# Shared PSUM banks, an earlier third pair of loads, and one more seven-part product in a fused retention and feed-forward kernel

**Chip, cores, metric.** One core of one Trainium2 chip. The time is the device time of a launch in microseconds (us); the kernel before takes 290.7 us.

## The reference

Retention (attention with a decay in place of the softmax) over 8 batches, 8 heads, 576 positions of 64 channels; its 4608 rows of 512 go through a feed-forward layer 512 -> 2048 -> 512 with a squared ReLU.

```python
scores = scale * np.matmul(q, k.transpose(0, 1, 3, 2))
Dmat = np.where(rel >= 0, gamma[:, None, None] ** rel[None, :, :], 0.0)
attn_out = np.matmul(scores * Dmat[None], v)
x = attn_out.transpose(0, 2, 1, 3).reshape(B * S, H * D)
h = x @ w_in
r = np.maximum(h, 0.0)
out = (r * r) @ w_out
```

## The kernel before

The rows are cut into 36 units of 128, two to a group: 18 groups. For each group TensorE computes the retention (scores `psc`, sums of the recurrent state `psS`, outputs `psO`: many small products with 64 rows), then the first feed-forward product (`ph`, 128x256 products) and the second (`po`). VectorE masks the scores, scales the outputs to `xT` and adds; ScalarE does ReLU and square; GpSimd casts the loaded q and v. The first eight units are loaded as four pairs (k0 to v6), between the eight weight blocks of 1 MB (w0 to w3 of `w_in`, w4 to w7 of `w_out`).

The order on every engine is fixed when the kernel is built. A small scheduler inside it walks through tasks with assumed durations, a key (smaller goes first), dependencies, and counts of buffers that a task must acquire:

```python
sched = Schedule(dict(ff=4, prS=1, prO=1, g=3, ld=5, wst=4, ...))
FIRST = ["k0","q0","v0","k2","q2","v2","w0","w1","w2","w3","w4","w5","w6","w7","k4","q4","v4","k6","q6","v6"]
```

The eight PSUM banks are four single ones for the feed-forward layer and two fixed pairs, one for scores and sums, one for outputs and sums:

```python
ps_ff  = ctx.enter_context(tc.tile_pool(name="ps_ff",  bufs=4, space=bass.MemoryType.PSUM))
ps_ret = ctx.enter_context(tc.tile_pool(name="ps_ret", bufs=1, space=bass.MemoryType.PSUM))
...
def emit_scores(g):
    tile_of["psc", g] = ps_ret.tile([P, 2, 512], FP32, name="psc", tag="prS")
    ...
def after_scores(g, t, key):                  # mask on VectorE, one unit of the group at a time
    for s, u in enumerate(units_of(g)):
        ...
        m = add("DVE", key + s, 0.7, fm, deps=[t] + ..., acq=("rT",))
    sched.free("prS", [m])
...
t = add("PE", base + 3, ..., fa, deps=scores_deps(g) + sums_deps(g), acq=("prS", "prO") if nf else ("prS",))
after_scores(g, t, base + 5)                  # a group whose scores are not joined to another's outputs
```

The loads wait for one another by a helper (`behind`), so that they share the transfers in a chosen order:

```python
if (name, u) == ("k", 4):
    behind(t, tile_of["w", 5])               # third pair's k is issued when w5 has landed
...
if i == 0:
    behind(tile_of["w", i], tile_of["load", "v", 0])
```

The second product has two forms. Up to group `STRASSEN` it is 16 products of 128x512 for each unit. From there on it is Strassen's seven half-size products instead of eight: seven parts of eight 128x256 products, for which VectorE forms sums `gS` of the activations and, once, differences `wT` of the weights. Each part adds into a bank a, b or c:

```python
if STRASSEN <= g:                             # STRASSEN = 2: groups 0 and 1 take the plain form
    add_strassen(g, us, base2, sq)
    return
...
def product(k, key, bank, left, right, deps, start, stop, reads):
    for q in range(4):
        def f(q=q):
            if start and q == 0:
                tile_of["pb", g, bank] = ps_ff.tile([P, HM], FP32, name="po", tag="ff")
            for i in (2 * q, 2 * q + 1):
                nc.tensor.matmul(tile_of["pb", g, bank], lhsT=left(i), rhs=right[:, i, :], ...)
        last[:] = [add("PE", base + key + q, 0.2184, f, deps=..., acq=("ff",) if start and q == 0 else ())]
```

## Time and profile before

| | before |
|---|---|
| time, median | 290.71 us (290.68 to 290.76) |
| span of the profiled run | 289.1 us |
| TensorE busy | 282.1 us, 98% |
| first feed-forward product starts | 17.74 us |
| last run of small products starts | 254.02 us |
| last run of products starts | 283.78 us |

TensorE is the bound; the lines are in the prediction below. "Busy" hides small gaps, since pipelined products overlap. So the accounts here use the timeline of TensorE: the start of one run of products minus the start of the next is what the first run cost, with all that it waited. Between fixed points of the same content (the start of the first feed-forward product at 17.74 us, and the end of the last run of small products at 254.95; some expectations below call this stretch "from 17.3") the kernel before takes 237.21 us: 209.65 are large products at 0.109 us for 256 columns and 0.216 for 512, with 32 transposes; 23.95 lie in 34 runs of small products; 3.74 are 34 times 0.11, the prediction's figure for what the return to large products costs, taken over and not measured one by one; nothing but rounding (-0.13) is left. A run of small products with the return to large ones is called an excursion.

### The profile page before, as it was taken

How to read it: one execution, taken by the hardware profiler on the slowest of the kernel's cores; microseconds unless marked ns; L12 is line 12 of the kernel's file. 1: busy time of each engine (PE TensorE's matmuls, PEld its weight loads, DVE VectorE, ACT ScalarE, POOL GpSimd, SP SyncE). 2: the span in 40 equal slices, each digit the busy share in tenths (PEclk: the TensorE clock that was granted, in tenths of full speed). 3: DMA queues.
4: the chain of work that ended last, by engine and by line, in shares of the span. 5: the costliest groups of instructions: out<-in, count | busy, mean ns of one | idle time of the engine just before them, and what ended most of it. 6: DMA issues, size and time to landing. Idle time of an engine off the chain costs nothing.

```text
span 289.1 us, 9988 instructions
## 1 busy us (share of the span) xinstructions
PE 282.1 (98%) x4322; PEld 234.3 (81%) x4322; DVE 182.4 (63%) x381; ACT 188.2 (65%) x361; POOL 84.1 (29%) x121
## 2 busy tenths in 40 slices
PE   8999999999999999999999999999999999999994
PEld 3568755788888888888888888888888888888883
DVE  3772368769585657736686857575777775455622
ACT  5459964685757676767756767676767676747830
POOL 5660035443333243342506061505250500000000
PEclk9999999999999999999999999999999999999999
DMA  7999999999999689999788799899995920201004
GB/s 202 274 208 206 249 291 267 219 203 202 221 188 198 153 201 199 217 219 219 154 199 168 172 194 205 163 196 206 225 182 151 181 76 2 75 2 73 2 8 139
DMA packets 139436, 49.94 MB, mean 173 GB/s; under 512 B 118144, under 2 KB 135040, under 8 KB 139392
## 3 DMA queue, kind: packets, MB, share of 16 engines
q1 hardware_dynamic: 134848, 44.84, 75.3%
q0 software_dynamic: 4224, 4.19, 8.8%
q8 instruction: 34, 0.56, 0.8%
q10 hardware_dynamic: 320, 0.26, 0.4%
q14 instruction: 10, 0.08, 0.1%
HBM read 36.70 MB, written 9.44 MB: 160 GB/s over the span
## 4 chain that ended last, share of the span: by engine, by line
PE 91%; DMA 3%; issue 2%; POOL 2%; DVE 0%; POOLq 0%; DVEq 0%
PE ph L859 44%; PE po L951 34%; PE po L899 5%; PE psO L345 4%; DMA w_in<-in_moe_w_in_dram 3%; PE psc L345 2%; PE psS L345 2%; PE psT L423 1%; POOL mask L215 0%; POOL vx L404 0%; POOL w_in L319 0%; DVE o L974 0%; POOL mask L207 0%; DVE p L1003 0%; POOL mask L211 0%
## 5 line engine op out<-in xcount | busy, mean ns | idle before, releaser
L859 PE MATMUL ph<-xT,w_in 128*128 128x256 f16 x1152 | 139.9, 273 | 0.1
L859 PEld LDWEIGHTS <-w_in 128*128 128x128 f16 x1152 | 110.9, 98 | 14.8 <-DMA w_in<-in_moe_w_in_dram 0.3
L867 ACT ACTIVATE rl<-ph 128x512 f16<-128x512 f32 x144 | 84.5, 588 | 52.5 <-PE ph L859 50.9
L877 ACT ACTIVATE gT<-rl 128x512 f16<-128x512 f16 x118 | 74.4, 631 | 3.4
L951 PEld LDWEIGHTS <-gS 128*128 128x128 f16 x512 | 49.8, 98 | 5.9
L951 PE MATMUL po<-wT,gS 128*128 128x256 f16 x384 | 52.1, 273 | 0.0
L928 DVE TENSOR_TENSOR gS<-gT,gS 128x512 f16<-128x512 f16 x64 | 32.8, 517 | 14.2 <-ACT gT L877 13.5
L951 PEld LDWEIGHTS <-gT 128*128 128x128 f16 x384 | 37.1, 98 | 4.5
L928 DVE TENSOR_TENSOR gS<-gT 128x512 f16<-128x512 f16 x64 | 30.9, 485 | 12.6 <-ACT gT L877 12.5
L359 POOL CAST kq<-k 128x512 f16<-128x512 f32 x28 | 18.6, 663 | 61.4 <-DMA k<-in_k_dram 60.2
L951 PE MATMUL po<-w_out,gT 128*128 128x256 f16 x256 | 34.7, 273 | 0.0
L371 POOL TENSOR_TENSOR v<-v,vdec_full 128x512 f16<-128x512 f32 x24 | 25.4, 1057 | 21.9 <-DMA v<-in_v_dram 20.9
L359 POOL CAST kq<-q 128x512 f16<-128x512 f32 x28 | 18.5, 660 | 30.8 <-DMA q<-in_q_dram 30.6
L964 ACT COPY u<-po 128x256 f32<-128x256 f32 x32 | 11.8, 369 | 19.1 <-PE po L951 18.9
L974 DVE TENSOR_TENSOR o<-po,u 128x256 f32<-128x256 f32 x31 | 13.0, 420 | 16.3 <-PE po L951 10.0
L736 DVE TENSOR_TENSOR xT<-psO,gam_full 128x512 f16<-128x512 f32 x28 | 18.1, 684 | 6.3 <-PE psO L345 6.2
L682 DVE TENSOR_TENSOR rT<-psc,mask 128x512 f16<-128x512 f32 x28 | 18.3, 683 | 4.6 <-PE psc L345 4.5
L879 DVE TENSOR_TENSOR gT<-rl 128x512 f16<-128x512 f16 x26 | 12.8, 492 | 12.6 <-ACT rl L867 11.9
L974 DVE TENSOR_TENSOR o<-po,p 128x256 f32<-128x256 f32 x17 | 7.2, 423 | 17.8 <-ACT u L964 8.8
L951 PE MATMUL po<-wT,gT 128*128 128x256 f16 x128 | 16.8, 273 | 0.0
L951 PE MATMUL po<-w_out,gS 128*128 128x256 f16 x128 | 16.8, 273 | 0.0
L899 PE MATMUL po<-w_out,gT 128*128 128x512 f16 x64 | 15.7, 380 | 0.0
(78 smaller groups left out, 224.0 us busy)
## 6 DMA issues: line engine op xcount, KB each, us to landing
out_dram<-o SPq DMA_DIRECT2D x32, 256.0 KB, 3.7
k<-in_k_dram SPq DMA_DIRECT2D x24, 256.0 KB, 4.8
q<-in_q_dram SPq DMA_DIRECT2D x24, 256.0 KB, 5.1
v<-in_v_dram SPq DMA_DIRECT2D x24, 256.0 KB, 4.9
pair<-in_k_dram SPq DMA_DIRECT2D x4, 512.0 KB, 7.0
pair<-in_q_dram SPq DMA_DIRECT2D x4, 512.0 KB, 7.2
pair<-in_v_dram SPq DMA_DIRECT2D x4, 512.0 KB, 7.0
w_in<-in_moe_w_in_dram POOLq DMA_DIRECT2D x4, 512.0 KB, 8.9
```

Source lines behind the costliest of these rows:

```text
L345: t = nc.tensor.matmul(out_, lhsT=lhsT, rhs=rhs, start=start, stop=True, skip_group_check=True, tile_position=(64 * row, 64 * col))
L359: op(out=out_.rearrange("p (n b a d) -> p n b a d", n=2, b=2, a=2), in_=in_.rearrange("p (n a b) d -> p n b a d", n=2, a=2))
L371: nc.gpsimd.tensor_tensor(out=t, in0=tile_of["v32", u], in1=vdec[kind].rearrange("p (h o) -> p h o", o=1).to_broadcast([P, H, D]), op=ALU. ...
L682: tile_of["masking", g] = nc.vector.tensor_tensor(out=r, in0=tile_of["psc", g][:, :, cols(s)].rearrange("p a (n i) -> p a n i", i=64), in1 ...
L736: nc.vector.tensor_tensor(out=tile_of["x", g][:, :, s * P:(s + 1) * P].rearrange("p n (c i) -> p c n i", c=2), in0=tile_of["psO", g][:, :, ...
L859: nc.tensor.matmul(tile_of["ph", g, fb][:, j, :], lhsT=w_in16[:, m, fi * P:(fi + 1) * P], rhs=tile_of["x", g][:, m, :], start=(m == 0), st ...
L867: nc.scalar.activation(out=t, in_=tile_of["ph", g, fb], func=ACTF.Relu)
L877: nc.scalar.activation(out=t, in_=rl, func=ACTF.Square)
L899: nc.tensor.matmul(tile_of["po", u], lhsT=tile_of["g", g][:, fi, s * P:(s + 1) * P], rhs=w_out16[:, fi, :], start=(fi == 0), stop=(fi == N ...
L928: nc.vector.tensor_tensor(out=Sx(k, h), in0=in0(h), in1=in1(h), op=op)
L951: nc.tensor.matmul(tile_of["pb", g, bank], lhsT=left(i), rhs=right[:, i, :], start=(start and i == 0), stop=(i == HF - 1), skip_group_chec ...
L974: nc.vector.tensor_tensor(out=o_tile(u)[:, half * HM:(half + 1) * HM], in0=bank(x), in1=tile_of[name, g], op=ALU.add)
```

## The change

The intent: one more group gets the cheaper second product; for that all eight weight blocks and their differences must be there while other work still fills TensorE, so the third pair's loads move ahead of w3; and any free PSUM bank may serve any purpose.

```diff
-    STRASSEN = 2
+    STRASSEN = 1
-    ps_ff  = ...tile_pool(name="ps_ff", bufs=4, space=PSUM)
-    ps_ret = ...tile_pool(name="ps_ret", bufs=1, space=PSUM)
+    ps_ff  = ...tile_pool(name="ps_ff", bufs=8, space=PSUM)
-    FIRST = [... "w0","w1","w2","w3","w4","w5","w6","w7","k4","q4","v4","k6","q6","v6"]
+    FIRST = [... "w0","w1","w2","k4","q4","v4","w3","w4","w5","w6","w7","k6","q6","v6"]
+    AFTER = {0: ("v", 0), 3: ("k", 4), ("k", 4): 0, ("k", 6): 5}   # who is issued behind whose landing
-    sched = Schedule(dict(ff=4, ..., rT=4, ...))
+    sched = Schedule(dict(ff=8, ..., rT=2, ...))
+    def banks(name):
+        return [ps_ff.tile([P, 512], FP32, name=name, tag="ff") for i in range(2)]
-            if (name, u) == ("k", 4):
-                behind(t, tile_of["w", 5])
+            if (name, u) in AFTER:
+                behind(t, tile_of["w", AFTER[name, u]])
-            if i == 0:
-                behind(tile_of["w", i], tile_of["load", "v", 0])
+            if i in AFTER:
+                behind(tile_of["w", i], tile_of[("load",) + AFTER[i]])
-        tile_of["psc", g] = ps_ret.tile([P, 2, 512], FP32, name="psc", tag="prS")
+        tile_of["psc", g] = banks("psc")
# after_scores: one mask per bank (both units), each frees its bank
-        for s, u in enumerate(units_of(g)):
+        for a in range(2):
+            m = add("DVE", key + a, 0.7, fm, deps=..., acq=() if a else ("rT",))
+            sched.free("ff", [m])
# (sums, outputs and their scaling likewise; acq lists gain "ff","ff" per pair of banks) ...
```

More of the change, by code (lines that the diff above doesn't have):

```diff
@@ L152 @@
     r_pool = ctx.enter_context(tc.tile_pool(name="r", bufs=3))
-    ps_ff = ctx.enter_context(tc.tile_pool(name="ps_ff", bufs=4, space=bass.MemoryType.PSUM))
-    ps_ret = ctx.enter_context(tc.tile_pool(name="ps_ret", bufs=1, space=bass.MemoryType.PSUM))
+    ps_ff = ctx.enter_context(tc.tile_pool(name="ps_ff", bufs=8, space=bass.MemoryType.PSUM))
     ctx.enter_context(tc.manual_schedule())
@@ L234 @@
     PAIRED = 8
-    SHARED = ()
-    FIRST = ["k0", "q0", "v0", "k2", "q2", "v2", "w0", "w1", "w2", "w3", "w4", "w5", "w6", "w7", "k4", "q4", "v4", "k6", "q6", "v6"]
-    sched = Schedule(dict(ff=4, prS=1, prO=1, g=3, ld=5, wst=4, kq=7, v16=7, rT=4, x=3, rl=3, o=4, p1=2, u2=2, u4=2,
+    FIRST = ["k0", "q0", "v0", "k2", "q2", "v2", "w0", "w1", "w2", "k4", "q4", "v4", "w3", "w4", "w5", "w6", "w7", "k6", "q6", "v6"]
+    AFTER = {0: ("v", 0), 3: ("k", 4), ("k", 4): 0, ("k", 6): 5}
+    sched = Schedule(dict(ff=8, prS=1, prO=1, g=3, ld=5, wst=4, kq=7, v16=7, rT=2, x=3, rl=3, o=4, p1=2, u2=2, u4=2,
                           R=5, Rm=2, kqT=6))
@@ L268, with dma_task @@
     tail_dec = add("DVE", 0, 0.3, lambda: make_vdec("tail", tile_of["iota_pt"]), deps=[tail_pool])
-    def dma_task(key, dur, fn, **kw):
-        t = add("SP", key, dur, fn, deps=list(last_load), **kw)
+    def dma_task(key, dur, fn, deps2=(), **kw):
+        t = add("SP", key, dur, fn, deps=list(last_load) + list(deps2), **kw)
         last_load[:] = [t]
@@ L304, in fn @@
             t = nc.sync.dma_start(out=x, in_=(k, q, v)[n][b, :, c * P:(c + 2) * P, :].rearrange("h (p e) d -> p h (e d)", e=2))
-            if (name, u) == ("k", 4):
-                behind(t, tile_of["w", 5])
+            if (name, u) in AFTER:
+                behind(t, tile_of["w", AFTER[name, u]])
             tile_of["load", name, u] = t
+        kw = dict(deps2=[wcast[AFTER[name, u]][0]]) if (name, u) in AFTER else {}
         loaded[name, u] = loaded[name, u + 1] = dma_task(0, 1.81 if loaded else 2.9, fn, acq=("wst",) if name != "q" else (),
-                                                         after=2.1 + LAG.get(name + str(u), 0.0))
+                                                         after=2.1 + LAG.get(name + str(u), 0.0), **kw)
     issues = []
@@ L319, in fn @@
             tile_of["w", i] = nc.gpsimd.dma_start(out=dst, in_=src)
-            if i == 0:
-                behind(tile_of["w", i], tile_of["load", "v", 0])
-        issue = add("POOL", -90 + i, 0.9, fn, deps=issues[-1:] or [loaded["v", 0]], lag=1.0 if issues else 0.0)
+            if i in AFTER:
+                behind(tile_of["w", i], tile_of[("load",) + AFTER[i]])
+        issue = add("POOL", -90 + i, 0.9, fn, deps=issues[-1:] + ([loaded[AFTER[i]]] if i in AFTER else []),
+                    lag=0.0 if i in AFTER else 1.0)
         issues.append(issue)
@@ L463, in fs @@
             def fs(e=e, tag=tag):
-                ps = rT["ps", e] = ps_ret.tile([P, 2, 512], FP32, name="psc", tag=tag)
+                ps = rT["ps", e] = banks("psc")
                 rT[e] = cast.tile([P, 2, NP, P], FP16, name="rx", tag="kq16")
@@ L467, in fs @@
                     for a, s in ((0, 0), (1, 1), (0, 1), (1, 0)):
-                        quad(ps[half(s), a, hp * P:(hp + 1) * P], kqT(s)[half(a), hp, half(e)], kqT(s)[half(a), NP + hp, :],
+                        quad(ps[a][half(s), hp * P:(hp + 1) * P], kqT(s)[half(a), hp, half(e)], kqT(s)[half(a), NP + hp, :],
                              a, s)
-            t = add("PE", base + 3 + e, 0.4, fs, deps=T["kqT", u] + T["kqT", u + 1], acq=(tag, "kq"))
+            t = add("PE", base + 3 + e, 0.4, fs, deps=T["kqT", u] + T["kqT", u + 1], acq=(tag, "kq", "ff", "ff"))
             ms = []
@@ L474, in fm @@
                     nc.vector.tensor_tensor(
-                        out=rT[e][:, a], in0=rT["ps", e][:, a].rearrange("p (n i) -> p n i", i=P),
+                        out=rT[e][:, a], in0=rT["ps", e][a].rearrange("p (n i) -> p n i", i=P),
                         in1=mask2[:, e].rearrange("p (o e) i -> p o (e i)", o=1).to_broadcast([P, NP, P]), op=ALU.mult)
-                def fc(e=e):
-                    nc.scalar.copy(out=rT[e][:, 1], in_=rT["ps", e][:, 1].rearrange("p (n i) -> p n i", i=P))
-                def fp(e=e):
-                    nc.gpsimd.tensor_tensor(
-                        out=rT[e][:, 1], in0=rT[e][:, 1],
-                        in1=mask2[:, e].rearrange("p (o e) i -> p o (e i)", o=1).to_broadcast([P, NP, P]), op=ALU.mult)
-                if a and g in SHARED:
-                    c = add("ACT", -60 + e, 0.66, fc, deps=[t])
-                    reads = ms + [c]
-                    ms.append(add("POOL", -60 + e, 0.75, fp, deps=[c]))
-                else:
-                    ms.append(add("DVE", base + 5 + e, 0.66, fm, deps=[t] + ms))
-                    reads = ms
-            sched.free(tag, reads)
+                ms.append(add("DVE", base + 5 + e, 0.66, fm, deps=[t] + ms))
+                sched.free("ff", ms[-1:])
+            sched.free(tag, ms)
             masked += ms
         def fk():
-            ps = rT["sum"] = [ps_ff.tile([P, 512], FP32, name="psS", tag="ff") for s in range(2)]
+            ps = rT["sum"] = banks("psS")
             for hp in range(NP):
@@ L541, in put2 @@
             col = h % 2
-            quad(tile_of["psO", g][half(col), s, 128 * (h // 2):128 * (h // 2) + 128], lhsT, rhs, row, col,
+            quad(tile_of["psO", g][s][half(col), 128 * (h // 2):128 * (h // 2) + 128], lhsT, rhs, row, col,
                  start=(g, s, col) not in begun)
@@ L546, in fo1 @@
         def fo1():
-            tile_of["psO", g] = ps_ret.tile([P, 2, 512], FP32, name="psO", tag="prO")
+            tile_of["psO", g] = banks("psO")
             for m in range(NP):
@@ L559, in fo2 @@
             inter(1)
-        t = add("PE", base + 23.9, 0.6, fo1, deps=masked + T["kvx", u], acq=("prO",))
+        t = add("PE", base + 23.9, 0.6, fo1, deps=masked + T["kvx", u], acq=("prO", "ff", "ff"))
         t = add("PE", base + 24, 0.75, fo2, deps=[t, T["R0", g]] + ([T["R", g - 1]] if carry else []))
@@ L574, in fx @@
                     out=tile_of["x", g][:, :, s * P:(s + 1) * P].rearrange("p n (i e) -> p n e i", e=2),
-                    in0=tile_of["psO", g][:, s].rearrange("p (n e i) -> p n e i", n=NP, e=2),
+                    in0=tile_of["psO", g][s].rearrange("p (n e i) -> p n e i", n=NP, e=2),
                     in1=gam_f.rearrange("p n (i e) -> p n e i", e=2), op=ALU.mult)
             T["x", u + s] = add("DVE", base + 25 + s, 0.7, fx, deps=[t] + ([T["x", u]] if s else []), acq=() if s else ("x",))
+            sched.free("ff", [T["x", u + s]])
         sched.free("prO", [T["x", u + 1]])
@@ L602, in emit_scores, with emit_sums @@
     def emit_scores(g):
-        tile_of["psc", g] = ps_ret.tile([P, 2, 512], FP32, name="psc", tag="prS")
+        tile_of["psc", g] = banks("psc")
         for s, u in enumerate(units_of(g)):
             kT = tile_of["kqT", u]
-            ps = tile_of["psc", g][:, :, cols(s)].rearrange("p a (n i) -> p a n i", i=64)
+            ps = [x[:, cols(s)].rearrange("p (n i) -> p n i", i=64) for x in tile_of["psc", g]]
             for hp in range(NP):
                 for a, c in ((0, 0), (1, 1), (0, 1), (1, 0)):
-                    quad(ps[half(c), a, hp, :], kT[half(a), hp, half(c)], kT[half(a), NP + hp, half(c)], a, c)
-    def emit_sums(g, tag):
+                    quad(ps[a][half(c), hp, :], kT[half(a), hp, half(c)], kT[half(a), NP + hp, half(c)], a, c)
+    def emit_sums(g):
         if not full_of(g):
             return
-        tile_of["psS", g] = ps_ret.tile([P, 2, 512], FP32, name="psS", tag=tag)
+        tile_of["psS", g] = banks("psS")
         for s, u in enumerate(units_of(g)):
@@ L619, in emit_sums @@
                 continue
-            ps = tile_of["psS", g][:, :, cols(s)].rearrange("p c (n i) -> p c n i", i=64)
+            ps = [x[:, cols(s)].rearrange("p (n i) -> p n i", i=64) for x in tile_of["psS", g]]
             for hp in range(NP):
@@ L623, in emit_sums @@
                     h = 4 * (hp // 2) + 2 * a + hp % 2
-                    quad(ps[half(a), c, hp, :], tile_of["kq", u][half(c), 0, half(2 * hp + a)],
+                    quad(ps[c][half(a), hp, :], tile_of["kq", u][half(c), 0, half(2 * hp + a)],
                          tile_of["v16", u][half(c), h, :], c, a)
@@ L633, in put @@
         s = units_of(g).index(u)
-        quad(tile_of["psO", g][half(col), c, 256 * s + 64 * (h // 2):256 * s + 64 * (h // 2) + 64], lhsT, rhs, row, col,
+        quad(tile_of["psO", g][c][half(col), 256 * s + 64 * (h // 2):256 * s + 64 * (h // 2) + 64], lhsT, rhs, row, col,
              start=(g, c, col) not in begun)
@@ L648, in emit_out1 @@
     def emit_out1(g):
-        tile_of["psO", g] = ps_ret.tile([P, 2, 512], FP32, name="psO", tag="prO")
+        tile_of["psO", g] = banks("psO")
         for u in units_of(g):
@@ L653, in emit_out2 @@
     def emit_out2(g):
-        for u in units_of(g):
+        for s, u in enumerate(units_of(g)):
             for m in range(NP):
@@ L658, in emit_out2 @@
                     put(g, u, c, h, tile_of["v16", u][half(c), h, :],
-                        tile_of["rT", u][half(c), m % 2, 2 * (m // 2) + b, :], c)
+                        tile_of["rT", g][half(c), s, m % 2, 2 * (m // 2) + b, :], c)
             inter(g, u, 0)
@@ L678, in after_scores, with fm @@
     def after_scores(g, t, key):
-        for s, u in enumerate(units_of(g)):
-            def fm(s=s, u=u):
-                r = tile_of["rT", u] = work.tile([P, 2, NP, 64], FP16, name="rT", tag="rT")
+        for a in range(2):
+            def fm(a=a):
+                if a == 0:
+                    tile_of["rT", g] = work.tile([P, 2, 2, NP, 64], FP16, name="rT", tag="rT", bufs=2)
                 tile_of["masking", g] = nc.vector.tensor_tensor(
-                    out=r, in0=tile_of["psc", g][:, :, cols(s)].rearrange("p a (n i) -> p a n i", i=64),
+                    out=tile_of["rT", g][:, :, a],
+                    in0=tile_of["psc", g][a].rearrange("p (s n i) -> p s n i", s=2, i=64),
                     in1=mask.rearrange("p (o r i) -> p o r i", o=1, r=1).to_broadcast([P, 2, NP, 64]), op=ALU.mult)
-            m = add("DVE", key + s, 0.7, fm, deps=[t] + (T["masked", g][-1:] if s else []), acq=("rT",))
+            m = add("DVE", key + a, 0.7, fm, deps=[t] + (T["masked", g][-1:] if a else []), acq=() if a else ("rT",))
+            sched.free("ff", [m])
             T.setdefault(("masked", g), []).append(m)
@@ L696, in fr0 @@
             r = tile_of["Rm", g] = st_pool.tile([P, 2, NP * D], FP16, name="Rm", tag="Rm", bufs=2)
-            x = tile_of["psS", g][:, 0]
+            x = tile_of["psS", g][0]
             if c0:
@@ L704, in fr1 @@
             r = tile_of["tmp", g] = work.tile([P, 2, NP * D], FP32, name="stmp", tag="stmp", bufs=1)
-            nc.vector.tensor_tensor(out=flat(r), in0=tile_of["psS", g][:, 1], in1=flat(tile_of["Rm", g]), op=ALU.add)
+            nc.vector.tensor_tensor(out=flat(r), in0=tile_of["psS", g][1], in1=flat(tile_of["Rm", g]), op=ALU.add)
         def fr2():
@@ L715, in after_sums @@
         T["Rm", g], T["R", g], T["Rread", g], T["Rmread", g] = r0, r2, [], r1
+        sched.free("ff", [r0])
+        sched.free("ff", [r1])
         sched.free(res, [r1])
@@ L723, in after_outs @@
             sched.free("v16", [t2])
-            sched.free("rT", [t2])
             for name, rg, at in states(u).values():
@@ L729, in after_outs, with fx @@
                     sched.free("Rm", [t2, T["Rmread", rg]])
-        for u in us:
-            s, at = groups[g].index(u), us.index(u)
-            def fx(s=s, at=at, u=u):
-                if ("x", g) not in tile_of:
+        sched.free("rT", [t2])
+        for c in range(2):
+            def fx(c=c):
+                if c == 0:
                     tile_of["x", g] = x_pool.tile([P, NP, n * P], FP16, name="xT", tag="xT")
                 nc.vector.tensor_tensor(
-                    out=tile_of["x", g][:, :, s * P:(s + 1) * P].rearrange("p n (c i) -> p c n i", c=2),
-                    in0=tile_of["psO", g][:, :, cols(at)].rearrange("p c (n i) -> p c n i", i=64),
-                    in1=gam[units[u][0]], op=ALU.mult)
-            T["x", u] = add("DVE", key + 0.1 * at, 0.7, fx, deps=[t2] + ([T["x", us[at - 1]]] if at else []),
-                            acq=() if at else ("x",))
-        sched.free("prO", [T["x", us[-1]]])
+                    out=tile_of["x", g].rearrange("p n (s c i) -> p c s n i", s=n, c=2)[:, c],
+                    in0=tile_of["psO", g][c].rearrange("p (s n i) -> p s n i", s=n, i=64),
+                    in1=gam[units[us[0]][0]][:, c].rearrange("p (s n) i -> p s n i", s=1).to_broadcast([P, n, NP, 64]), op=ALU.mult)
+            x = add("DVE", key + 0.1 * c, 0.7, fx, deps=[t2] + ([x] if c else []), acq=() if c else ("x",))
+            sched.free("ff", [x])
+        for u in us:
+            T["x", u] = x
+        sched.free("prO", [x])
     def add_casts(g):
@@ L762, in fa @@
                 emit_scores(g)
-                emit_sums(g, "prO")
+                emit_sums(g)
             t = add("PE", base + 3, 0.2 + 16 * QUAD * (n + nf), fa, deps=scores_deps(g) + sums_deps(g),
-                    acq=("prS", "prO") if nf else ("prS",))
+                    acq=("prS", "ff", "ff") + (("prO", "ff", "ff") if nf else ()))
             for u in units_of(g):
@@ L777, in f2 @@
             def f2():
-                emit_sums(g + 1, "prS")
-                if not full_of(g + 1):
-                    first_waits.append(tile_of["masking", g + 1])
+                first_waits.append(tile_of["masking", g + 1])
+                emit_sums(g + 1)
                 emit_out2(g)
             t1 = add("PE", base + 10, 0.2 + QUAD * (8 * n + 16 * k), f1, deps=out1_deps(g) + scores_deps(g + 1),
-                     acq=("prO", "prS"))
+                     acq=("prO", "prS", "ff", "ff", "ff", "ff"))
             after_scores(g + 1, t1, base + 11)
             t2 = add("PE", base + 30, 0.2 + QUAD * (24 * n + 16 * len(full_of(g + 1))), f2,
-                     deps=[t1] + T["masked", g] + T["masked", g + 1] + sums_deps(g + 1), acq=("prS",) if full_of(g + 1) else ())
+                     deps=[t1] + T["masked", g] + T["masked", g + 1] + sums_deps(g + 1), acq=("prS", "ff", "ff") if full_of(g + 1) else ())
             for u in units_of(g + 1):
@@ L797, in add_ret @@
             t = add("PE", base + 24, 0.45 + 32 * QUAD * n, fb, deps=T["masked", g] + out1_deps(g),
-                    acq=("prO",))
+                    acq=("prO", "ff", "ff"))
             after_outs(g, t, t, base + 27)
```

## The prediction

> **What bounds the kernel now.** I read the page's first part, then the busy time by stage, then the chain of work from 17 to 61 us, then the timelines of VectorE, GpSimd and the SyncE queue at the start.
>
> ```profile
> PE 282.1 (98%) x4322; PEld 234.3 (81%) x4322; DVE 182.4 (63%) x381; ACT 188.2 (65%) x361; POOL 84.1 (29%) x121
> ```
>
> TensorE is busy 98% of the span; no other engine is over 65%. By stage (columns: stretch, its length, busy us of PE, PEld, DVE, ACT, POOL with instruction counts, clock, DMA share, GB/s):
>
> ```profile
> 0.00:17.74 17.74, 15.78 (x234) 8.13 (x235) 11.56 (x51) 8.57 (x19) 11.34 (x29) 1.00 1.04 233
> 17.74:60.30 42.56, 42.23 (x560) 30.22 (x554) 23.42 (x40) 31.86 (x58) 11.30 (x15) 1.00 1.15 237
> 60.30:119.80 59.50, 59.21 (x965) 51.35 (x963) 42.74 (x77) 40.99 (x79) 23.75 (x30) 1.00 1.06 201
> 119.80:284.50 164.70, 164.60 (x2574) 144.55 (x2574) 104.00 (x214) 106.78 (x207) 37.70 (x48) 1.00 0.69 141
> ```
>
> Until 17.74 us loads set the pace and TensorE does filler ("warm") products between the first two pairs. From 17.74, when the first feed-forward product starts, to 284.0, when the last one ends, it hardly idles; 5 us of last additions and stores follow. So the time is start-up (17.7) + TensorE's own work + what it waits (266.3 together) + tail. Only a change in TensorE's work or a stall counts. Some pieces of the chain (start, length, what; one piece of it runs to the next):
>
> ```profile
> 28.94 2.18 PE ph L859 x20
> ...
> 35.90 4.32 PE po L899 x20
> ...
> 43.05 0.38 PE psS L345 x32
> ...
> 43.97 0.57 PE psc L345 x32
> ...
> 49.35 1.19 PE po L899 x5
> 50.53 0.35 PE psc L345 x16
> ```
>
> These give the units. A 128x256 product costs 2.18/20 = 0.109 us, a 128x512 one 4.32/20 = 0.216. A run of small 64-row attention products costs a fixed part and a part each: 0.57 for 32 against 0.35 for 16 is 0.0138 each and 0.13 fixed. The five large products after one such run took 1.19 against 5 x 0.216 = 1.08, another 0.11. So each excursion from large to small products and back costs 0.24 us beside its content.
>
> **Is there idle time to win?** From 17.74 to 60.46: 192 products of 128x256 (20.98), 64 of 128x512 (13.82), 32 transposes (0.45 per 8: 1.8), 200 small products of 128 columns (2.75), 64 of 64 columns at 0.0078 ((0.38-0.13)/32; 0.5), six excursions (1.44): 41.3 of 42.7. The rest, 1.4, is mostly three drains inside the pairs' outputs (some 0.3 each) and 0.1 at the second weight block; only some 0.3 is plain waiting. From 60.46 on: 1856 large products 202.8, 1680 small 13.2, 28 excursions 6.7, four drains 0.7: 223.4 of 223.5. The steady state has nothing to win.
>
> **What the Trainium skill says.** "TensorE: Matmul & The Clock Gate", section "Wait — 56ns, not 53.3ns?", gives N / 2.4 GHz + 2.5 ns: 109 and 216 ns for 256 and 512 columns; the trace agrees to the nanosecond. "TensorEngine Tiling (Array Packing)", Key Properties: "Mode switching requires drain"; the 0.24 us above are that in this trace. "PSUM — Partial Sum Buffer", Specifications (TRN2): 8 banks per partition of 512 fp32; before, they were 4 shared single ones and two fixed pairs, after, 8 shared ones, so the change adds no bank, only freedom. "DMA: Bandwidth & Descriptors", Queues, rings and completion order: each DMA engine round-robins between the queues. The trace agrees only loosely: the third pair's k, issued at 29.9 beside two pending weight blocks, let them land first (below).
>
> **The change, part by part.** (1) Second product of group 1 in seven parts: 32 x 0.216 = 6.91 us become 56 x 0.109 = 6.12: **-0.8 us**, all on the bounding engine. Its eight sum operations on VectorE (0.48 each, 4 us) and some copies on ScalarE lie beside it. It needs all eight weight blocks and their differences.
>
> (2) Order of instructions, which building the changed kernel shows without running it. The excursions go from 39 to 43: five before the first feed-forward product in both, six then ten in the stretch with pairs three and four (scores in halves, outputs in two pieces), 28 afterwards in both. 4 x 0.24: **+1.0 us**. The splitting may hide part of a drain or the 0.3 us of waiting: **-0.3**.
>
> (3) Third pair's loads. Before, they wait for the sixth weight block:
>
> ```profile
> 29.90 0.37 SPq L304 DMA_DIRECT2D pair<-in_k_dram  x1
> ```
>
> On VectorE the landings of w5, w6 and w7 can be read:
>
> ```profile
> 29.86 0.69 DVE L811 TENSOR_TENSOR wT<-w_out 128x1024 f16<-128x1024 f16 x1 [0.70 <-DMA w_out<-in_moe_w_out_dram]
> ...
> 32.44 0.69 DVE L811 TENSOR_TENSOR wT<-w_out,wT 128x1024 f16<-128x1024 f16 x1 [1.88 <-DMA w_out<-in_moe_w_out_dram]
> ...
> 35.57 0.69 DVE L811 TENSOR_TENSOR wT<-w_out,wT 128x1024 f16<-128x1024 f16 x1 [2.44 <-DMA w_out<-in_moe_w_out_dram]
> ```
>
> A weight block every 2.6 us or so, 3.1 with a pair in between; and GpSimd shows the third pair's q at 38.8, its v by 40.5: 1.8 us each. So k landed some 6.9 us after its issue. Afterwards k is issued when w0 lands (about 17.2), again beside two pending blocks: w1 19.7, w2 22.5, k 24, q 26, v 28. w3 is issued only when k has landed; w0, issued with pair two pending, came some 3.3 us after that pair's v, so w3 comes at 28 + 3 = 31, then w4 33.5, w5 36, w6 38.5, w7 41.2. Total DMA work is the same.
>
> Would TensorE stall for w3? The built order says no: after w2's 20 products it does 36 of group 1 (they need only w0 to w2), the third pair's transposes, 8 more, the sums, 4 more, and only then group 0's fourth block. From 22.3: 2.2 + 3.9 + 0.9 + 0.9 + 0.5 + 0.4 = 31.1, just as w3 is due. Walking on in the same way, w4 is asked for at 34.2, w5 at 36.3, w6 at 38.5, w7 at 41.5: everywhere within a microsecond of its landing. A planned fit, with little margin: **+0 to 2 us of stalls, some 0.4 expected**. The seven-part product of group 1 is reached at about 51 us, ten after w7, so the weight differences (eight operations, 6.2 us) are in time.
>
> (4) The shared banks: the masks now go over one bank of both units instead of both banks of one unit, the same 512 elements, 0.68 us each. In the steady state the order has the same excursions (48 small products, 20 large ones, 80 small ones), so **0**.
>
> Sum: -0.8 + 1.0 - 0.3 + 0.4 = +0.3, 291.0; without any stall 290.6. Such an order is only chosen if it paid in its author's trials, and my 0.24 per excursion is the weakest term (an excursion whose waiting hides under the drain is cheaper). I therefore set 290.5.
>
> **Rivals.** A, ScalarE as the bound at the start: between 19 and 36 us it is busy without a gap (0.58 + 0.63 per bank against TensorE's 0.87 for its eight products). Before, second products filled the difference; afterwards TensorE does 84 first products in a row and only the eight banks carry it. By my count up to four banks are filled and unread at 31 us, with four more held by transposes and sums: just enough. If not, TensorE stops 1 to 2 us: 291.5 to 292.5. B, the w3 wait: if k lands 3 us late, its casts, which stand before later activations in ScalarE's order, hold up everything, and w3 with it: 3 us, 293. Against it: the same situation gave 6.9 us before. C, loads hidden and drains hidden by the splitting, so that seven parts pay in full: 289.8. For it: large products now stand between the two halves of the outputs. D, the shared banks shorten steady-state waits, some us: against it, there are none (0.1 us left over in 223).
>
> **Range and chances.** Almost all of the time is fixed work of one engine, so over 2% faster (284.9) would need more idle time than exists, and over 2% slower needs a 5.8 us stall in the start. C and a hidden drain give the low end, A and part of B the high end: 289.6 to 292.0. Faster 0.01, within 2% 0.97, slower 0.02.
>
> **What would show it.** Right: 896 + 56 = 952 of the 128x256 second products and 32 of the 128x512; the first feed-forward product again near 17.7; TensorE waiting for w3 under 1 us near 31; group 2's second product starting near 60 us, as before (60.3); from there to the end the same 224 us within 0.3. Wrong: an idle TensorE of over 1 us between 22 and 45 us (A, B), a steady period other than 14.6 us per group (D), or excursions costing under 0.15 us.

## The result, and the profile after

The changed kernel takes **292.68 us** in the median (292.40 to 293.26, four runs), the kernel before beside it 290.69 (290.56 to 290.76, four runs). The ratio is 1.0072, 95% interval 1.0054 to 1.0089. (A ratio here is the mean time of one kernel's fast runs over that of the other's of the same rounds, so not quite the ratio of the medians.) That is within 2%, as was given 97%, but 0.7 us above the top of the range, and slower by 2.0 us where the number said 0.2 faster.

The page's first part, then busy time by stage, both of the changed kernel, in the columns of the prediction:

```profile
PE 282.5 (97%) x4346; PEld 235.7 (81%) x4346; DVE 185.2 (64%) x392; ACT 188.4 (65%) x363; POOL 85.1 (29%) x121
```

```profile
17.70:60.30 42.60, 41.32 (x566) 30.72 (x564) 29.03 (x52) 32.08 (x60) 14.82 (x18) 1.00 1.14 222
60.30:119.80 59.50, 58.62 (x951) 50.91 (x952) 38.06 (x74) 38.48 (x74) 22.43 (x29) 1.00 1.01 205
```

TensorE has 1.28 us of gaps in the first stretch, where it had 0.33, and 0.88 in the second, where it had 0.29. Nothing is lost later. The view of TensorE's waits from 17 to 100 us, which holds no line for the kernel before, has two for the changed one (total, times, longest):

```profile
PE ph L856 <- DMA w_in<-in_moe_w_in_dram: 0.8, 1, 0.8
PE po L948 <- DVE rT L676: 0.6, 1, 0.6
```

TensorE's timeline at the start (start, length, engine and line, operation, out<-in, shapes, count, and in brackets idle time and its releaser):

```profile
30.11 0.45 PE L349 MATMUL psS<-vx,kx 64*64 64x64 f16 x32
30.49 0.61 PE L856 MATMUL ph<-xT,w_in 128*128 128x256 f16 x4
31.89 1.92 PE L856 MATMUL ph<-xT,w_in 128*128 128x256 f16 x16 [0.80 <-DMA w_in<-in_moe_w_in_dram]
...
39.41 5.47 PE L896 MATMUL po<-w_out,gT 128*128 128x512 f16 x23
44.71 1.91 PE L856 MATMUL ph<-xT,w_in 128*128 128x256 f16 x16
...
47.78 0.86 PE L427 MATMUL psT<-ident,qx 128*128 128x128 f16 x8
48.47 2.35 PE L856 MATMUL ph<-xT,w_in 128*128 128x256 f16 x20
```

Four products from 30.49 should end at 30.93, but the next, the first to need w3, starts at 31.89: 0.96 us. The 23 products from 39.41 should take 4.97 us and take 5.30: 0.33, for the last two blocks of `w_out` (they land at about 39.6 and 42.7; the product that reads the last one starts at 42.77). Third, eight transposes of the fourth pair's q at 47.78 take 0.69 us, where the same eight take 0.45 elsewhere: 0.24. They wait for GpSimd's casts of that q, two in 2.08 us here and in 1.17 in the kernel before, so this is only in part a matter of loads. Together 1.53 us, 1.29 of them for weight blocks. The cause of the first can be followed back on the SyncE queue and GpSimd, one fence each:

```profile
17.22 0.37 SPq L306 DMA_DIRECT2D pair<-in_k_dram  x1
```

```profile
24.50 0.81 POOL L322 DMA_DIRECT2D w_in<-in_moe_w_in_dram  x1 [8.90 <-DMA pair<-in_k_dram]
26.16 0.60 POOL L412 CAST qx<-pair 128x512 f16<-128x512 f32 x1 [0.85 <-DMA pair<-in_q_dram]
26.71 0.75 POOL L322 DMA_DIRECT2D w_out<-in_moe_w_out_dram  x1
27.45 0.62 POOL L412 CAST qx<-pair 128x512 f16<-128x512 f32 x1
28.03 1.05 POOL L408 TENSOR_TENSOR vx<-pair,vdec_pair 128x512 f16<-128x512 f32 x1
29.02 2.30 POOL L322 DMA_DIRECT2D w_out<-in_moe_w_out_dram  x3
```

The k is issued at 17.22, when w0 has landed; it lands 7.0 us later, at 24.2, and lets w3 go at 24.50; w3 lands 7.3 us after that, at about 31.8, and its products start at 31.89.

GpSimd's timeline shows more: w4 is issued at 26.71, behind a cast of the third pair's q, and w5 to w7 from 29.02 on, behind the product that waits for its v. Before, the last four blocks were issued in a row from 16.34:

```profile
16.34 2.98 POOL L319 DMA_DIRECT2D w_out<-in_moe_w_out_dram  x4
```

From 26 to 32 us, when both kernels load mostly weight blocks, the views by stage (columns as in the prediction) show 206 GB/s for the kernel before and 165 for the changed one:

```profile
26.00:32.00 6.00, 6.00 (x49) 4.62 (x48) 1.72 (x3) 5.87 (x11) 0.00 (x0) 1.00 1.24 206
```

```profile
26.00:32.00 6.00, 5.21 (x84) 4.34 (x82) 3.30 (x4) 4.92 (x10) 5.16 (x7) 1.00 1.15 165
```

So the blocks come late not only because they stand behind the pair: the transfers themselves run slower meanwhile. The late issues are the likely reason; no run tested it.

The fourth wait is of another kind. TensorE, then VectorE, around 81 us:

```profile
80.91 0.60 PE L948 MATMUL po<-wT,gS 128*128 128x256 f16 x4
82.09 1.03 PE L948 MATMUL po<-w_out,gT 128*128 128x256 f16 x8 [0.59 <-DVE rT L676]
```

```profile
80.27 0.83 DVE L925 TENSOR_TENSOR gS<-gT 128x512 f16<-128x512 f16 x1
81.03 0.41 DVE L925 TENSOR_TENSOR gS<-gT,gS 128x512 f16<-128x512 f16 x1
81.36 0.68 DVE L676 TENSOR_TENSOR rT<-psc,mask 128x512 f16<-128x512 f32 x1
```

Four products from 80.91 end at 81.35; the next start at 82.09: 0.74 us. They open a new accumulator, bank b of the seven-part product. The eight banks were last given to accumulators a and c, two of scores, two of sums, two feed-forward blocks. Which of them b gets is fixed when the kernel is built, and building it shows that b gets a scores bank. That one is free once VectorE's mask has read it, and the mask stands in VectorE's order behind the sums `gS`. One feed-forward block's bank was free 1.2 us earlier, since ScalarE had read it by 80.83, but the built program does not look for it:

```profile
80.23 0.60 ACT L864 ACTIVATE rl<-ph 128x512 f16<-128x512 f32 x1 [1.17 <-PE ph L856]
```

Before, scores had their own pair, and b took one of the four feed-forward banks.

Finally the same account for both kernels, in us, from the first feed-forward product to the end of the last run of small products (17.68 to 257.01 us in the changed kernel):

| | large products | runs of small products | returns | waits and rest | total |
|---|---|---|---|---|---|
| before | 209.65 | 23.95 in 34 | 3.74 | -0.13 | 237.21 |
| after | 208.86 | 24.20 in 38 | 4.18 | 2.09 | 239.33 |
| difference | -0.79 | +0.25 | +0.44 | +2.22 | +2.12 |

The returns are counted (four more at 0.11), so an error in them would stand under waits and rest. The same loss can be read without this account. Group 2's second product starts at 61.76 us instead of 60.30, 1.46 later; from there to the start of the last run of products both kernels have the same products, and it takes 224.08 us instead of 223.48, 0.60 more: the first three waits lie before that point, the bank wait after it.

### The profile page after: what moved, and what is told of

It is laid out like the page before. It is cut to its first block, busy times and chain, and to the rows that moved or that the text cites.

```text
span 291.1 us, 10058 instructions
## 1 busy us (share of the span) xinstructions
PE 282.5 (97%) x4346; PEld 235.7 (81%) x4346; DVE 185.2 (64%) x392; ACT 188.4 (65%) x363; POOL 85.1 (29%) x121
## 4 chain that ended last, share of the span: by engine, by line
PE 70%; DVE 1%; issue 0%; DVEq 0%
PE ph L856 34%; PE po L948 31%; PE psO L349 3%; PE psS L349 1%; PE psc L349 1%; DVE o L971 0%; DVE rT L676 0%; DVE p L1000 0%; DVEq L971 0%
## 5 line engine op out<-in xcount | busy, mean ns | idle before, releaser
L948 PEld LDWEIGHTS <-gS 128*128 128x128 f16 x544 | 52.5, 98 | 6.4
L948 PE MATMUL po<-wT,gS 128*128 128x256 f16 x408 | 54.9, 273 | 0.0
L925 DVE TENSOR_TENSOR gS<-gT 128x512 f16<-128x512 f16 x68 | 35.5, 524 | 15.6 <-ACT gT L874 15.6
L948 PEld LDWEIGHTS <-gT 128*128 128x128 f16 x408 | 39.3, 98 | 5.6 <-issue 0.8
L925 DVE TENSOR_TENSOR gS<-gT,gS 128x512 f16<-128x512 f16 x68 | 31.0, 459 | 12.5 <-ACT gT L874 10.6
L948 PE MATMUL po<-w_out,gT 128*128 128x256 f16 x272 | 36.7, 273 | 0.6 <-DVE rT L676 0.6
L971 DVE TENSOR_TENSOR o<-po,u 128x256 f32<-128x256 f32 x33 | 13.9, 421 | 15.9 <-PE po L948 9.6
L948 PE MATMUL po<-w_out,gS 128*128 128x256 f16 x136 | 18.2, 273 | 0.0
L948 PE MATMUL po<-wT,gT 128*128 128x256 f16 x136 | 17.7, 273 | 0.0
L478 DVE TENSOR_TENSOR rx<-psc,mask 128x512 f16<-128x512 f32 x16 | 10.1, 683 | 3.7 <-PE psc L349 3.7
```

The costliest lines, as they stand in the source:

```text
L925: nc.vector.tensor_tensor(out=Sx(k, h), in0=in0(h), in1=in1(h), op=op)
L971: nc.vector.tensor_tensor(out=o_tile(u)[:, half * HM:(half + 1) * HM], in0=bank(x), in1=tile_of[name, g], op=ALU.add)
```

## The experiments

The first eight runs take the change apart; the times of the kernel before beside them were 290.64 (290.50 to 290.89) and 290.73 (290.47 to 290.87).

**1. Seven parts alone** (the kernel before with one number changed):

```diff
-    STRASSEN = 2
+    STRASSEN = 1
```

> The kernel before with the second product of group 1 in seven parts and nothing else. Theory (the seven parts save 0.8 us of TensorE, but need the third pair's data and the weight differences early, so the loads had to move with them): TensorE runs out of work near 38 us, 3 to 5 us idle, 293 to 295 us. Rival (the seven parts pay by themselves and the new load order is what costs): 290 us.

Measured: 298.02 us (297.25 to 298.31), ratio 1.0248 [1.0229, 1.0266]. The two longest of its TensorE waits from 17 to 62 us:

```profile
PE psc L345 <- DVE xT L573: 2.0, 1, 2.0
PE psS L345 <- POOL vx L404: 1.1, 1, 1.1
```

The cheaper product saves its 0.79 in the account (208.86 of large products) and 5.3 us of waits and 2.4 us of longer small runs come with it. The plain product of group 1 had been the filling between the third and fourth pair's small products; the seven-part one can't start before all weights are there, and the pairs' chain through VectorE and GpSimd lies bare.

**2. The load order alone** (the kernel before with the new `FIRST` and `AFTER`):

```diff
-    FIRST = [... "w2","w3","w4","w5","w6","w7","k4","q4","v4", ...]
+    FIRST = [... "w2","k4","q4","v4","w3","w4","w5","w6","w7", ...]
+    AFTER = {0: ("v", 0), 3: ("k", 4), ("k", 4): 0, ("k", 6): 5}
```

> The kernel before with the new order of loads alone. 40 excursions to small products against 39. Theory (the wait for the fourth weight block, 0.9 us, and smaller ones are the loads' doing): 291.5 to 292.3 us with a TensorE wait for a weight block near 30 us. Rival (the waits come from the bank sharing, which moved the products): 290.7 to 291.0.

Measured: 295.65 us (295.31 to 295.97), ratio 1.0171 [1.0156, 1.0186]; worse than either theory said. Its two longest waits in the same stretch:

```profile
PE po L902 <- DMA w_out<-in_moe_w_out_dram: 2.1, 3, 1.2
PE ph L862 <- DMA w_in<-in_moe_w_in_dram: 0.6, 1, 0.6
```

**3. The shared banks alone** (the changed kernel with the old loads and `STRASSEN = 2`):

```diff
-    STRASSEN = 1
+    STRASSEN = 2
-    FIRST = [... "w2","k4","q4","v4","w3", ...];  AFTER = {0: ("v", 0), 3: ("k", 4), ("k", 4): 0, ("k", 6): 5}
+    FIRST = [... "w2","w3", ... "w7","k4","q4","v4", ...];  AFTER = {0: ("v", 0), ("k", 4): 5}
```

> Shared single banks alone: the changed kernel with the old order of loads and group 1 in one piece. 39 excursions. Theory (the wait of 0.6 us near 81 us, for a bank that a mask on VectorE has not freed, comes from sharing): 290.7 to 291.5 us, TensorE waiting for VectorE's mask once or more. Rival (sharing gives freedom and helps): 290.0 to 290.5.

Measured: 291.84 us (291.69 to 292.14), ratio 1.0042 [1.0027, 1.0057]. The bank wait is here without any change of loads or products, on its TensorE timeline:

```profile
64.76 0.60 PE L948 MATMUL po<-wT,gS 128*128 128x256 f16 x4
66.04 1.03 PE L948 MATMUL po<-w_out,gT 128*128 128x256 f16 x8 [0.68 <-DVE rT L676]
```

From 65.20 (64.76 + 4 x 0.109) to 66.04: 0.84 us. Step (4) of the prediction, "**0**", is wrong.

**4. All but the seven parts** (the changed kernel, `STRASSEN = 2`).

```diff
-    STRASSEN = 1
+    STRASSEN = 2
```

> The changed kernel with group 1 in one piece: new loads and shared banks. 40 excursions. Theory (+0.2 for an excursion, +0.9 wait for the fourth weight block, perhaps +0.6 bank wait): 291.6 to 292.4, so the seven parts as such neither won nor lost much. Rival (the seven parts caused the loss): 290.7 to 291.0.

Measured: 292.52 us (291.77 to 292.86), ratio 1.0060 [1.0044, 1.0076]: beside the changed kernel's 292.68 the seven parts change nothing that the spread could show. By the account, this run's trace has 0.79 more in large products than the changed kernel's, some 0.6 less in its three fewer excursions, and 0.88 less in waits and rest (no bank wait shows in it; against the second look at the changed kernel, number 16, the waits differ by 0.50). So what the seven parts save goes into switching, and their share of the waits is not settled by one trace.

**5. w3 issued behind w1 instead of behind the third pair's k** (the changed kernel):

```diff
-                behind(tile_of["w", i], tile_of[("load",) + AFTER[i]])
+                behind(tile_of["w", i], tile_of["w", 1] if i == 3 else tile_of[("load",) + AFTER[i]])
```

> The changed kernel; the fourth weight block is issued when the second has landed and no longer when the third pair's k has. Same instruction order on every engine. Theory (TensorE waited 0.9 us near 31 us for this block and nothing else): that wait goes; the third pair's q and v land up to 2 us later, and TensorE may wait for them near 29 us; net 291.7 if they are hidden. Rival (the DMA engines are full from 8 to 45 us, so that the wait only changes its name): 292.5 to 293.5, with a wait for the third pair in its place.

Measured: 293.77 us (293.65 to 294.30), ratio 1.0108 [1.0093, 1.0123], slower still. TensorE's timeline:

```profile
29.59 1.04 PE L856 MATMUL ph<-xT,w_in 128*128 128x256 f16 x8
31.73 0.45 PE L349 MATMUL psS<-vx,kx 64*64 64x64 f16 x32 [1.10 <-POOL vx L408]
```

The wait for w3 is gone, and in its place stands one of 1.27 us for the third pair's v. The rival's outcome came (a wait with another name, 0.3 us above its range), but not for its reason, full DMA engines: GpSimd now issues w4 at 27.94 and w5 to w7 from 31.63, later than before this edit, and between 28 and 30 us the transfers run at 82 GB/s:

```profile
28.00:30.00 2.00, 1.88 (x26) 1.63 (x24) 0.00 (x0) 1.99 (x4) 1.30 (x2) 1.00 0.51 82
```

So it is not the position of one issue: the blocks behind it wait for the pair on GpSimd all the same.

**6. The mask earlier in VectorE's order** (the changed kernel, groups whose scores are not joined):

```diff
-            after_scores(g, t, base + 5)
+            after_scores(g, t, base - 15)
```

> The changed kernel with the masks of the groups that are not joined given an earlier key on VectorE, ahead of the sums for the seven parts. Theory (TensorE waited 0.6 us near 81 us for a bank that the mask frees): that wait goes, 292.1. Rival (the sums that are pushed back are then what TensorE waits for): 292.7 or more with a wait for a sum.

Measured: 292.52 us (292.16 to 292.88), ratio 1.0061 [1.0046, 1.0076]. The bank wait is gone, as TensorE's timeline shows:

```profile
82.03 0.60 PE L948 MATMUL po<-wT,gS 128*128 128x256 f16 x4
82.47 1.04 PE L948 MATMUL po<-w_out,gT 128*128 128x256 f16 x8
```

Four products at 0.109 are 0.44: no gap; the masks now run at 78.80. The cause of that wait is settled, but the median fell by only 0.16. In its trace the account's stretch is 1.13 us shorter, but it starts 0.32 later (18.00 us), and the kernel's tail is longer, which is taken up under numbers 13 to 16.

**7. A pair's two halves of scores in one run** (changed kernel; four banks at once, two excursions fewer):

```diff
-            t = add("PE", base + 3 + e, 0.4, fs, deps=..., acq=(tag, "kq", "ff", "ff"))
+            if e == 0:
+                t = add("PE", base + 3, 0.8, <both halves>, deps=..., acq=("prS", "prO", "kq", "kq", "ff", "ff", "ff", "ff"))
```

> The changed kernel with both halves of a pair's scores as one task that takes four banks at once. 41 excursions to small products instead of 43, and another order around them. Theory (an excursion costs 0.24 us wherever it stands): 0.5 us less of it, 292.2 if no new wait comes; the sum of TensorE's runs shows the 0.24 in any case. Rival (the excursion's cost was hidden under waiting): no gain.

Measured: 297.75 us (296.08 to 299.56), ratio 1.0243 [1.0197, 1.0289]. It brought new waits (1.8 us for `rx`, 1.7 for `w_out`, 1.4 for the fourth pair's q) and so tells nothing about an excursion's price.

**8. Load order and seven parts, old banks** (run 2 with `STRASSEN = 1`):

```diff
-    STRASSEN = 2
+    STRASSEN = 1
```

> The kernel before with the new loads and the seven parts, but its fixed pairs of banks. 42 excursions. Theory (-0.8 for the seven parts, +0.7 for three excursions, +1 of waits on weight blocks, no bank wait): 291.6 to 292.2, so 0.5 to 1 us under the changed kernel. Rival (sharing the banks is what makes the load order bearable): over 293.

Measured: 295.63 us (294.77 to 296.70), ratio 1.0158 [1.0134, 1.0183]; 2.8 us wait for `w_out` in its trace, 1.1 for ScalarE's `rl`. With shared banks this is the changed kernel, 2.95 us faster. So the parts are not a sum: the times of the medians are

| shared banks | new load order | seven parts | us |
|---|---|---|---|
| - | - | - | 290.7 |
| yes | - | - | 291.8 |
| - | yes | - | 295.7 |
| - | - | yes | 298.0 |
| yes | yes | - | 292.5 |
| - | yes | yes | 295.6 |
| yes | yes | yes | 292.7 |

Each part alone loses, and each combination that was run loses less than its parts added up (shared banks and load order 1.8 against 1.1 + 5.0). Shared banks make the new load order bearable: with them the waits of run 2 shrink. What stays is a loss.

The next four ran beside 290.74 (290.41 to 290.88).

**9 and 10. One weight block less to load.** w3 is copied from w2 on VectorE: a wrong result on purpose (relative error 0.64), everything else the same. Number 9 is the changed kernel with this, number 10 adds the early mask of number 6.

```diff
+            if i == 3:
+                tile_of["w", i] = nc.vector.tensor_copy(out=dst, in_=w_in16[:, :, 1024:1536])
+                return
             tile_of["w", i] = nc.gpsimd.dma_start(out=dst, in_=src)
# number 10 only
-            after_scores(g, t, base + 5)
+            after_scores(g, t, base - 15)
```

> The changed kernel, wrong on purpose: the fourth weight block is copied on VectorE from the third, so 1 MB of reads is gone from the full DMA engines; the products' order is that of the changed kernel. Theory (the start is bound by the transfers: waits for w3 0.96, w6 or w7 0.33, q of pair four 0.24 us in the profiled run): all of them go, 1.5 us less, 291.2. Rival (the order of the products, with its four excursions, is what costs): 292.4 to 292.8.

> The same wrong kernel with the masks of the groups that are not joined ahead on VectorE as well. Theory (the account is complete: transfers 1.5, the bank that waits for a mask 0.7): 290.5 us, the time of the kernel before, since the seven parts' 0.8 and four excursions' 0.7 cancel. Rival (the mask's key moved the wait elsewhere): as without it, 291.2.

Measured: 291.88 us (291.60 to 292.21), ratio 1.0042 [1.0025, 1.0059], and 291.38 (290.74 to 291.58), ratio 1.0018 [1.0003, 1.0033]. In number 9 the run of 20 that broke for w3 is whole:

```profile
30.37 2.36 PE L859 MATMUL ph<-xT,w_in 128*128 128x256 f16 x20
```

The waits on `w_out` and the fourth pair's q are gone with it, and of the account's waits only the bank's 0.80 is left; the stretch takes 237.70 us, 1.63 less than in the changed kernel, as the theory had it. With the early mask that goes too: the stretch takes 236.88 us, 0.33 less than before, and the view of waits is empty. The medians missed the theories all the same, 291.88 for 291.2 and 291.38 for 290.5; numbers 13 to 16 look for the difference. And the DMA engines were not full here: with w3 gone they moved 24 GB/s from 26 to 28 us, until w4, issued at 26.61, got going. What the run shows is that the blocks' lateness costs the 1.5 us, not that their bytes must.

**11. Shared banks alone, mask early** (number 3 with the line of number 6).

```diff
-            after_scores(g, t, base + 5)
+            after_scores(g, t, base - 15)
```

> Shared banks alone (old loads, group 1 in one piece) with the masks ahead. Shared banks alone took 291.8, with 0.84 us of wait for a bank in the profiled run. Theory: that wait goes, 290.9 to 291.1. Rival (sharing costs elsewhere): 291.6 to 292.

Measured: 291.34 us (290.91 to 291.78), ratio 1.0021 [1.0006, 1.0036]. Where number 3 waited, its timeline runs on, 0.44 us for four products:

```profile
64.93 0.60 PE L948 MATMUL po<-wT,gS 128*128 128x256 f16 x4
65.37 1.04 PE L948 MATMUL po<-w_out,gT 128*128 128x256 f16 x8
```

**12. The price of an excursion, by itself** (the kernel before; from group 8 on the sums and the outputs, which go in one run, are set apart: eight excursions more, no other work added):

```diff
-            t2 = add("PE", base + 30, ..., f2, deps=..., acq=("prS",) ...)
+            t1b = add("PE", base + 30, ..., lambda: emit_sums(g + 1, "prS"), deps=..., acq=("prS",))
+            t2 = add("PE", base + 30, ..., lambda: emit_out2(g), deps=[t1b], lag=0.3)
```

> The kernel before with the sums of the joined groups parted from the outputs that followed them, four large products between: 47 excursions to small products instead of 39, nothing else. Theory (0.24 us each, as read from the chain): +1.9 us, 292.6. Theory from the totals of the two kernels (0.17 each): +1.4, 292.1. Rival (the large product hides it): 290.7.

Measured: 292.52 us (291.99 to 292.63), ratio 1.0058 [1.0043, 1.0073]. +1.78 us over eight is 0.22 us each; the trace gives 1.72. One of the eight places, on TensorE's timeline:

```profile
202.92 1.04 PE L863 MATMUL ph<-xT,w_in 128*128 128x256 f16 x8
204.17 0.45 PE L345 MATMUL psS<-v,kq 64*64 64x64 f16 x32 [0.21 <-DVE rT L682]
204.55 0.61 PE L863 MATMUL ph<-xT,w_in 128*128 128x256 f16 x4
```

This place also shows the only wait it added, 0.2 us for a mask; 0.31 us of the 1.72 are waits, so an excursion by itself is 0.18 to 0.22. The prediction's 0.24 less some hiding stands.

**13 to 16. Second looks.** The variants without waits still had medians 0.6 us above the kernel before, and their profiled runs were their fastest. So two of them, and the changed kernel, were looked at again, unchanged (13 and 14 are number 11, 15 is number 10, 16 is the changed kernel; the kernel before beside them took 290.54).

> Same kernel as the shared banks with the early mask, looked at again because its one profiled run (290.91) was the fastest of four (median 291.34). Theory: the other runs are slower by a wait of TensorE for a bank or a mask that moves with the arrival of the loads, so a look at 291.2 or more shows 0.3 to 0.8 us of idle TensorE before the last run of small products that the first look (236.74 us from 17.3) did not have, at a line that reads a bank. Rival: the difference lies in the start before 17.3 us or in the tail after the last product; then the stretch again takes 236.7 to 236.9 while the time is 291.2 or more.

> As the look before it: a time between 290.9 and 291.8; whatever exceeds 290.9 is, by the theory, idle TensorE between 17.3 us and the last run of small products, by the rival start or tail.

> The copied w3 with the early mask (wrong result on purpose), looked at again: its profiled run (290.74) was the fastest of four (median 291.38). Theory: a slower look shows 0.3 to 0.8 us of idle TensorE in the stretch that took 236.88 us at the first look; rival: the same stretch takes 236.9 within 0.1 and the start or tail is longer.

> The changed kernel looked at again: 292.4 to 293.3. Theory of this study: the same four waits as in the first profile (w3 0.96 near 31 us, second products 0.33 near 39 us, the fourth pair's q 0.24 near 47 us, the bank 0.74 near 82 us), 2.2 us together; each within 0.4 of that, and the sum within 0.6, or the account rests on one accidental trace.

Measured: 291.07, 291.36, 291.20 and 292.42 us. From the first feed-forward product to the start of the last run of small products the three looks at number 11 took 235.82, 235.95 and 236.39 us, and the kernel before 236.28: TensorE ends there as early. What sets their times above the kernel before's lies mostly behind that point. From the start of VectorE's last addition to the end of the span the kernel before takes 4.21 us, the changed one 4.14 and 4.15, numbers 3, 4, 5 and 12 4.12 to 4.20; but numbers 6, 9, 10, 11, 13, 14 and 15 take 4.44 to 4.66, and 1, 2, 7 and 8 4.48 to 4.63 (spans are read to 0.1 us, so each figure is good to 0.05). In each of these eleven the DMA view shows a transfer of the kind "instruction" between 4.4 and 5.0 us after that addition, which is within some 0.3 us of the span's end, before it or after; in the other seven there is none at that place (number 4 has one 5.6 us after, past its end). For number 11, from 288 us to the end, it is the only transfer:

```profile
q14 instruction: 1, 0.01, 0.5%
```

So the rival of numbers 13 to 15 is right for about 0.4 us, which the early mask happens to bring along, as do other edits (number 9 has it without the mask; all of them change the order of instructions, none the tail's work), and the theory for the rest: number 14 lost 0.30 us to number 13 at the sums between 47 and 50 us, in the loads' stretch. Whether that transfer is what lengthens the tail was not tested; it is seen beside the longer tail each time, not shown to cause it.

Number 16 corrects this study's own account. Its timeline of TensorE:

```profile
30.54 2.36 PE L856 MATMUL ph<-xT,w_in 128*128 128x256 f16 x20
...
36.72 1.24 PE L896 MATMUL po<-w_out,gT 128*128 128x512 f16 x5 [0.24 <-DMA w_out<-in_moe_w_out_dram]
...
40.00 5.00 PE L896 MATMUL po<-w_out,gT 128*128 128x512 f16 x22 [0.65 <-DMA w_out<-in_moe_w_out_dram]
```

The wait for w3, 0.96 us in the first trace, is not there at all, and two waits for `w_out` of some 0.4 and 0.8 us stand in its place. By 50.6 us this run is only 0.19 us better off (0.12 earlier, after a start 0.07 later). The bank wait is there again, 0.53 instead of 0.74. "The same four waits" failed, the sum held: some 1.3 us for loads in one trace and 1.5 (with the casts of q) in the other, whichever block is the late one.

## Why the prediction was wrong

Its steps in order:

- **(1) Seven parts: -0.8.** Right: large products fell from 209.65 to 208.86 us, 952 products of 128x256 and 32 of 128x512 as counted.
- **(2) Four more excursions: +1.0, less 0.3 hidden.** Right: 0.25 in the runs, measured, and 0.44 in the returns, counted, are +0.69, against 0.7, and number 12 measured the price by itself, 0.18 to 0.22. The doubt cast on the 0.24 ("the weakest term") was put on the wrong term.
- **(3) Loads moved: "+0 to 2 us of stalls, some 0.4 expected".** The step that failed: 1.5 us were lost here, 1.3 of them waiting for weight blocks. Its times for the pair came out well: k landed at 24.2 (said 24), v was used at 28.0 (said 28), and w3 was asked for at 30.9 (said 31.1). Its times for the blocks did not: w3 to w7 landed at about 31.8, 34.4, 37.1, 39.6 and 42.7, where it had 31, 33.5, 36, 38.5 and 41.2, so 0.8 to 1.5 us late. It let the blocks follow v every 2.5 us as before, and did not ask when GpSimd would issue them (26.71 for w4, from 29.02 for the rest). And it took a plan in which five blocks in a row arrive "within a microsecond" of their need as costing 0.4. A row of near ties costs the latest of them, since TensorE once delayed asks later for the next but the transfers are as late as before: w7 landed 1.2 us after the 41.5 at which the step has it asked for, and 1.3 is what all blocks together cost. Numbers 5 and 9 show it: moving w3 forward moves the wait to the third pair's v; taking 1 MB of transfers away removes it. Whether issuing w4 to w7 ahead of GpSimd's casts would remove it too was not run.
- **(4) Shared banks: "0".** Wrong by 0.5 to 0.8 us. The step looked at the number of excursions and the cost of a mask, and asked of no bank who frees it. Numbers 3 and 6 show the new dependence: bank b of the seven-part product waits for a mask on VectorE, because the build gave it the bank of those scores.
- **The last step, from 291.0 down to 290.5.** The reason was that "such an order is only chosen if it paid in its author's trials". That is no evidence from the profile, and it took the number away from what the sum said. The kernel's own scheduler, when the kernels are built, has TensorE's last task end at 286.54 in the changed order against 286.67. The sum of its assumed TensorE durations falls by the full 0.80, so it charges nothing for the four excursions, nor for loads that come late, which is what decided here.
- **Rivals.** B (the w3 wait) was the right place with too large a size and too strict a cause: k came on time. A did not happen: no wait for ScalarE between 22 and 45 us. C failed: loads were not hidden, and the four excursions cost 0.7, the 0.3 that was hidden being all the help. D failed, as argued: there was nothing to shorten; the shared banks lengthened instead. Of the signs, the counts, the start near 17.7 and a w3 wait under 1 us (0.96) came; group 2's second product at 61.76 instead of "near 60", and 0.60 more from there on instead of "within 0.3", did not. Of its signs of being wrong one came: TensorE idle for over 1 us between 22 and 45 us (1.29).

With 1.5 in place of 0.4 and 0.7 in place of 0, the sum is -0.8 + 1.0 - 0.3 + 1.5 + 0.7 = +2.1; measured +2.0.

Open: whether earlier issues of w4 to w7 would save the load waits, whether old loads, shared banks and seven parts together would do better (not run), what makes the tail of eleven profiles 0.4 us longer, and the last few tenths of number 11. No version run here beats the kernel before; 290.7 stands.

## What to carry to other kernels

When a plan has several transfers in a row due just as they are needed, charge it the largest likely lateness of the row, not the mean of one, and look up on the issuing engine's timeline what stands ahead of each issue; test it by taking bytes away, since reordering one issue may only move the wait. When buffers become shared, list for every acquire the buffer that the build gives it, the engine whose release it now waits for, and what stands ahead of that release in its order. Parts of a change that open room for one another can't be judged alone, and a part that saves a known amount (0.79 us here) may spend it on switching.

## What the Trainium skill lacked or had wrong

- "TensorEngine Tiling (Array Packing)", Key Properties, says that switching modes needs a drain, without a size. Here one excursion from 128-row to 64-row products and back costs 0.18 to 0.22 us beside its content (eight of them: 1.78 us); that the drain is what it pays for, as the prediction takes it, is not shown.
- "DMA: Bandwidth & Descriptors", Queues, rings and completion order, has the engines go round between queues. It gives no help for a load issued beside pending weight blocks: the third pair's k took 7.0 us from issue to landing, as estimated from the kernel before (6.9), and w3 was first used at 31.9 us after a wait in one run of the changed kernel, and by 31.0 without one in another.
- "PSUM — Partial Sum Buffer", Specifications, counts the eight banks, which agrees; no page was found that warns that a common pool ties a bank to another engine's order, 0.5 to 0.8 us here.
- No page was found that ties the length of a kernel's end to a transfer of instructions: eleven profiles with one within 0.3 us of the end have a tail of 4.44 to 4.66 us, seven without have 4.12 to 4.21.
